# Attention and feed-forward layer on one core: the last chunk's stores as one transfer per queue and tile for two blocks of 32 rows

## The chip, the core and the metric

The kernel runs on one core of a Trainium2 chip. Its engines work side by side: TensorE (PE in the profile, its weight loads PEld) multiplies matrices, VectorE (DVE) and ScalarE (ACT) work on tiles, GpSimd (POOL) does a few small things, and SyncE (SP) issues transfers. A transfer (DMA) is issued by SP or ACT, goes into that engine's DMA queue and is carried out by the core's 16 DMA engines, between the memory on the chip (128 partitions) and the large memory outside. In the profile SP's queue is q1 and ACT's is q10.

The metric is the device time of one execution in microseconds (us), as the median of several runs. A difference of 0.2% is about what can be told apart here.

## The reference, cut to what matters

There are 8 batches, 8 heads, 32 global and 512 local positions, a head dimension of 64 and a model width of 512. The global queries attend to all 544 positions, the local ones to the global ones and to a band of 32 to each side. A layer with normalization and two matrices follows, on all 8 x 544 rows of 512 numbers:

```python
    out_g = np.matmul(sm(s_g), v_all)                                  # 32 global rows per batch
    out_l = np.matmul(a_l, np.concatenate([v_g, v_l], axis=2))         # 512 local rows per batch
    attn_out = np.concatenate([out_g, out_l], axis=2)                  # global rows stand first
    x = attn_out.transpose(0, 2, 1, 3).reshape(B, S, H * D)
    xn = (x - mu) / np.sqrt(var + 1e-06) * g_ln
    ch = np.maximum(xn @ w_ch1, 0.0) @ w_ch2
    return (x + ch).astype(np.float32)
```

The lines are put together from the reference's functions. The output has the shape 8 x 544 x 512. So the 32 global rows of one batch are one run of 64 KB in memory, and from one batch's to the next batch's there are 544 rows.

## The kernel before, in words

The work goes in nine chunks. Eight of them hold 512 local rows each, as four tiles of 128 rows. The last chunk holds the global rows of all 8 batches: 256 rows, as two tiles of 128, and each tile is four blocks of 32 rows from four batches. While the feed-forward part of one chunk runs, the attention of the next one runs beside it.

The feed-forward part (class `Ffn`) takes 16 steps. In each, `first` multiplies the normalized rows with a piece of the first matrix (L830, into `ph`), ScalarE and VectorE make the hidden values in two parts (L839, L843), and `second` adds their product with a piece of the second matrix to `acc` (L855), one `acc` for each tile of rows.

At a chunk's end, tile by tile: `residual` has loaded the rows of x from the scratch tensor `xs` into `ob` some time before, `add` (L867, VectorE) adds `acc` to `ob`, and `store` (L869 to L875) sends `ob` to the output. In the wide chunks a tile is one block of 128 rows and one transfer on SP's queue (by `dma`, L407). In the last chunk `rows_global` lists four blocks of 32 rows for a tile, and `store` is called twice: with `part` 0 it takes the first two blocks (partitions 0 to 63) on SP's queue, with `part` 1 the other two (partitions 64 to 127) on ACT's queue (L875). Each block is a transfer of its own, 64 KB.

The order of instructions on each engine is written out in a table by operation number. A call of `store` is one operation in it, whatever number of transfers it issues, so the change leaves the table as it is. Nothing follows the last stores but the end of the program.

Of the kernel before, what the change touches and what calls it, by code (L numbers as in the profile page):

```python
# [319 lines left out]
def attention_ffn_kernel(  # L320
# [12 lines left out]
    nc = tc.nc  # L333
# [4 lines left out]
    SA = gk.shape[4] - SG  # L338
# [34 lines left out]
    for sgn in (1, -1):  # L373
        nc.gpsimd.affine_select(
            out=band,
# [30 lines left out]
    def dma(to, src):  # L406
        nc.sync.dma_start(to, src)  # L407
# [104 lines left out]
    class Local:  # L512
# [116 lines left out]
        def store(self, j):  # L629
            b, _, half = self.at  # L630
            r0 = b * SA + SG + half * 256 + j * P
            dma(xs[r0:r0 + P, :], self.x[:, j, :])
# [179 lines left out]
    out_flat = out.rearrange("b s d -> (b s) d")  # L812

    class Ffn:
# [54 lines left out]
        def store(self, t, part=0, parts=1):  # L869


            n = len(self.rows[t]) // parts
            for ps, r0, nr in self.rows[t][part * n:part * n + n]:
                if part:
                    nc.scalar.dma_start(out_flat[r0:r0 + nr, :], self.ob[ps, t, :])  # L875
                else:
                    dma(out_flat[r0:r0 + nr, :], self.ob[ps, t, :])

    def open_pool(name):
        cm = tc.tile_pool(name=name, bufs=1, reuse_waits="tile")  # L880
# [686 lines left out]
```

## Time and profile before

| what | value |
|---|---|
| runs | 904.42, 905.08, 905.54 us; median 905.08 |
| the profiled execution's own time | 905.45 us |
| its span, first to last instruction | 903.6 us |
| PE busy | 889.5 us, 98% of the span |
| DVE, ACT, POOL busy | 694.8, 311.0, 40.6 us |
| mean granted TensorE clock | 0.994 of full speed |
| memory read and written | 100.67 and 17.83 MB |

The span leaves out what lies around the first and the last instruction, 1.85 us here. Busy shares are means over the whole program; the chain of waits says what is on the path to the end. A DMA's share is that of 16 engines: 100% means that all 16 were busy.

### The profile page before, as it was taken

Reading aid. Unit: us, or ns where it says so; the run is one execution under the profiler, and the core shown is the slowest. Engines: PE = TensorE matmul, PEld = TensorE weight load, DVE = VectorE, ACT = ScalarE, POOL = GpSimd, SP = SyncE. Lnnn points to the kernel's source line nnn. Section 1 sums busy time; section 2 is a strip of 40 time slices with the busy share of each in tenths; the row PEclk is TensorE's granted clock in tenths of the full one; section 3 lists DMA queues with packets and bytes.
Section 4 is the critical chain, followed back from the end, with each engine's and each line's share of the span. In section 5 each row is a group of like instructions: output and inputs, shape, how many; then the busy total and the mean of one; then the engine's idle time right before and its main releaser. Section 6 shows DMA issues by size and latency. Waiting matters only on the chain.

```text
span 903.6 us, 21437 instructions
## 1 busy us (share of the span) xinstructions
PE 889.5 (98%) x8517; PEld 707.2 (78%) x8517; DVE 694.8 (77%) x2448; ACT 311.0 (34%) x880; POOL 40.6 (4%) x133
## 2 busy tenths in 40 slices
PE   7899999999999999999999999999999999999997
PEld 4588787877788887778877787878887777777896
DVE  5899999789878888788878896888876287766411
ACT  7798873232223222322322222322323122222211
POOL 4100100000000000000000000000000000000000
PEclk9899999999999999999999999999999999999999
DMA  9696836324134313324332403332331426445200
GB/s 347 251 333 207 284 110 210 101 79 148 47 104 147 118 38 125 102 78 148 120 101 83 148 16 110 118 117 92 125 102 53 155 101 238 162 176 204 68 15 24
DMA packets 42868, 119.88 MB, mean 133 GB/s; under 512 B 5136, under 2 KB 7184, under 8 KB 40720
## 3 DMA queue, kind: packets, MB, share of 16 engines
q1 hardware_dynamic: 42576, 118.25, 37.9%
q8 instruction: 67, 1.10, 0.5%
q14 instruction: 33, 0.27, 0.1%
q10 hardware_dynamic: 192, 0.26, 0.1%
HBM read 100.67 MB, written 17.83 MB: 131 GB/s over the span
## 4 chain that ended last, share of the span: by engine, by line
PE 83%; DVE 2%; issue 0%
PE ph L830 37%; PE acc L855 37%; PE sc L548 3%; PE pv L603 3%; PE pv L739 1%; PE sc L662 1%; DVE pt L595 1%; PE tp L710 0%; DVE xl L808 0%; DVE ob L867 0%; PE t L790 0%; DVE w L462 0%; DVE hl L843 0%; DVE tmp L452 0%; DVE tmp L446 0%
## 5 line engine op out<-in xcount | busy, mean ns | idle before, releaser
L855 PE MATMUL acc<-w,hh 128*128 128x512 f32 x1088 | 342.0, 395 | 0.0
L830 PE MATMUL ph<-xh,w 128*128 128x512 f32 (+1 forms) x1216 | 308.2, 379 | 0.8 <-DVE hl L843 0.6
L830 PEld LDWEIGHTS ph<-xh,w 128*128 128x128 f32 x1216 | 215.5, 188 | 49.0 <-DVE hl L843 1.1
L855 PEld LDWEIGHTS acc<-w,hh 128*128 128x128 f32 x1088 | 204.9, 188 | 47.4
L839 ACT ACTIVATE hh<-ph 128x512 fp32r<-128x512 f32 (+1 forms) x144 | 82.9, 576 | 438.9 <-PE ph L830 409.1
L855 PE MATMUL acc<-w,hl 128*128 128x512 f32 x544 | 218.5, 402 | 0.0
L595 DVE STREAM_TRANSPOSE pt<-p 32x128 f32<-32x128 f32 x768 | 207.2, 289 | 9.5 <-ACT p L572 1.1
L843 DVE SCALAR_TENSOR_TENSOR hl<-ph,hh 128x512 fp32r<-128x512 f32 (+1 forms) x144 | 95.2, 661 | 120.0 <-ACT hh L839 119.0
L830 PE MATMUL ph<-xl,w 128*128 128x512 f32 x512 | 141.1, 397 | 0.0
L572 ACT ACTIVATE p<-p,mn 128x128 f32<-128x128 f32 x256 | 99.8, 392 | 92.5 <-DVE mn L560 92.4
L855 PEld LDWEIGHTS acc<-w,hl 128*128 128x128 f32 x544 | 102.1, 188 | 23.3
L830 PEld LDWEIGHTS ph<-xl,w 128*128 128x128 f32 x512 | 95.7, 188 | 23.8 <-DVE xl L808 0.2
L798 DVE STREAM_TRANSPOSE tmp<-x 32x128 f32<-32x128 f32 x320 | 96.7, 302 | 4.8
L560 DVE CUSTOM_DVE_ANT_0 p<-sc,mask 128x128 f32<-128x128 f32 x256 | 61.0, 284 | 21.7 <-PE sc L548 21.3
L572 ACT ACTIVATION_READ_ACCUMULATOR p<-p,mn 128x1 f32 x256 | 48.4, 189 | 0.0
L615 POOL TENSOR_SCALAR ri<-sm 128x4 f32<-128x4 f32 x64 | 16.9, 264 | 639.9 <-ACT p L572 638.1
L722 DVE STREAM_TRANSPOSE gpt<-gp 32x128 f32<-32x128 f32 x144 | 43.5, 302 | 2.3
L622 DVE TENSOR_TENSOR x<-pv,ri 128x256 f32<-128x256 f32 x64 | 24.8, 418 | 13.8 <-PE pv L603 13.8
L548 PEld LDWEIGHTS sc<-u_e 64*32 64x32 f32 x1792 | 24.9, 105 | 10.2 <-issue 8.8
L548 PE MATMUL sc<-u_e 64*32 64x128 f32 x1792 | 32.4, 274 | 0.0
L603 PE MATMUL pv<-u_v,pt 128*32 128x64 f32 x1792 | 30.8, 220 | 0.0
L603 PEld LDWEIGHTS pv<-u_v,pt 128*32 128x32 f32 x1792 | 26.3, 110 | 5.7 <-issue 5.7
(71 smaller groups left out, 501.7 us busy)
## 6 DMA issues: line engine op xcount, KB each, us to landing
u_v<-in_ev SPq DMA_DIRECT2D x56, 512.0 KB, 4.9
u_e<-in_eq SPq DMA_DIRECT2D x56, 336.0 KB, 6.2
raw<-in_wd SPq DMA_DIRECT2D x32, 512.0 KB, 7.4
gk<-in_gk SPq DMA_DIRECT2D x8, 1152.0 KB, 6.3
xs<-x SPq DMA_DIRECT2D x32, 256.0 KB, 6.3
ob<-xs SPq DMA_DIRECT2D x32, 256.0 KB, 5.6
out<-ob SPq DMA_DIRECT2D x32, 256.0 KB, 3.7
gv<-in_gv SPq DMA_DIRECT2D x8, 1024.0 KB, 5.0
```

Of the source, the lines that this page charges most:

```text
L548: nc.tensor.matmul(sc[h][gp, qb * P:(qb + 1) * P], self.e[hd, w * WIN:(w + 1) * WIN], self.e[hd, k0 * WIN:(k0 + 4) * WIN], start=True, sto ...
L560: nc.vector.tensor_tensor_reduce(out=self.p[:, c], in0=self.sc[h][:, qb * P:(qb + 1) * P], in1=masks[self.at[2], qb], scale=-QSCALE, scala ...
L572: nc.scalar.activation(self.p[:, c], self.p[:, c], AF.Exp, bias=self.mn[:, c:c + 1], scale=-1.0, accum_out=self.sm[:, c:c + 1],)
L595: nc.vector.transpose(out=self.pt[rp, :, gp], in_=self.p[gp, :, rp])
L603: nc.tensor.matmul(pv[gp, qb * P + h * D:qb * P + h * D + D], self.pt[:, 2 * h + qb, gp], self.v[:, 4 * qb + g, h * D:(h + 1) * D], start= ...
L622: nc.vector.tensor_tensor(self.x[:, :, hp * P:(hp + 1) * P].rearrange("p q (h d) -> p q h d", h=2), self.pv[:, :256].rearrange("p (q h d) ...
L722: nc.vector.transpose(out=self.pt[rp, h, :n, ip], in_=p[ip, :, r])
L798: nc.vector.transpose(out=dst[rp, 2 * half:2 * half + 2, :, i], in_=src[ip, :, k:k + 2, r])
L830: nc.tensor.matmul(self.ph[f][:, :self.n], w[:, kt, :], xx[kt][:, :self.n], start=begins and kt == 0, stop=ends and kt == KT - 1,)
L839: nc.scalar.activation(hh[:, :self.n], self.ph[f][:, :self.n], AF.Relu)
L843: nc.vector.scalar_tensor_tensor(hl[:, :self.n], self.ph[f][:, :self.n], 0.0, f32(hh[:, :self.n]), ALU.max, ALU.subtract,)
L855: nc.tensor.matmul(self.acc[t], a[:, ts], w, start=(f == 0 and i == 0), stop=(f == NF - 1 and i == 2),)
```

## The change

In the last chunk, one call of `store` issues one transfer for its two blocks of 32 rows. The destination is addressed as a piece of the output of 2 batches x 32 rows x 512, the source as 64 partitions x 512. SP and ACT still take two blocks of a tile each. For a tile with one block (the wide chunks) the transfer is what it was.

```diff
             n = len(self.rows[t]) // parts
-            for ps, r0, nr in self.rows[t][part * n:part * n + n]:
-                if part:
-                    nc.scalar.dma_start(out_flat[r0:r0 + nr, :], self.ob[ps, t, :])
-                else:
-                    dma(out_flat[r0:r0 + nr, :], self.ob[ps, t, :])
+            ps, r0, nr = self.rows[t][part * n]
+            if n == 1:
+                to, ob = out_flat[r0:r0 + nr, :], self.ob[ps, t, :]
+            else:
+                b = r0 // SA
+                to = out[b:b + n, :nr, :]
+                ob = self.ob[ps.start:ps.start + n * nr, t, :]
+            (nc.scalar.dma_start if part else dma)(to, ob)
```

On SP's queue the end of the program reads so (`-` before, `+` changed; `out` is the output, `ob` the tile of sums, `xs` the scratch tensor; the sizes are those of the destination, and in brackets stand the semaphores that an instruction waits for, those of DMA queues and VectorE's):

```order
 L407 DMA ob<-xs 32x512 [waits DMAHW4_49]
 L407 DMA ob<-xs 32x512 x4
-L407 DMA out<-ob 32x512 [waits DMAHW2_49,DMAHW1_49,DVE_49]
-L407 DMA out<-ob 32x512 [waits DMAHW3_49]
-L407 DMA out<-ob 32x512 [waits DMAHW5_49,DVE_49]
-L407 DMA out<-ob 32x512 [waits DMAHW7_49,DMAHW6_49]
-L1563 UNCONDITIONAL_BRANCH
+L407 DMA out<-ob 2x32x512 [waits DMAHW2_49,DMAHW1_49,DVE_49]
+L407 DMA out<-ob 2x32x512 [waits DMAHW5_49,DMAHW6_49,DMAHW3_49,DVE_49]
+L1566 UNCONDITIONAL_BRANCH
```

Four transfers with two waits for VectorE's additions have become two with one such wait each, and the destination has three dimensions where it had two.

On ACT's queue, behind the last activations of the hidden values:

```order
 L839 ACTIVATE hh<-ph 128x256 [waits DVE_49,PE_49] x15
-L875 DMA out<-ob 32x512 [waits DMAHW3_49,DMAHW1_49,DVE_49]
-L875 DMA out<-ob 32x512 [waits DMAHW4_49]
-L875 DMA out<-ob 32x512 [waits DMAHW7_49,DMAHW6_49,DVE_49]
-L875 DMA out<-ob 32x512 [waits DMAHW0_49]
-L1563 UNCONDITIONAL_BRANCH
+L880 DMA out<-ob 2x32x512 [waits DMAHW3_49,DMAHW4_49,DMAHW1_49,DVE_49]
+L880 DMA out<-ob 2x32x512 [waits DMAHW7_49,DMAHW0_49,DVE_49]
+L1566 UNCONDITIONAL_BRANCH
```

The same has happened here, and the line of the issue is now L880. No other instruction of any engine has moved.

## Rows read from the trace of the kernel before

**Rows 1.** Page, busy time by engine and the chain by engine.

```profile
PE 889.5 (98%) x8517; PEld 707.2 (78%) x8517; DVE 694.8 (77%) x2448; ACT 311.0 (34%) x880; POOL 40.6 (4%) x133
...
PE 83%; DVE 2%; issue 0%
```

**Rows 2.** Chain in order of time, its end: start us, us, what.

```profile
896.02 2.82 PE acc L855 x12
898.84 0.02 issue
898.86 0.69 DVE ob L867
```

**Rows 3.** Timeline from 890: start us, us, engine, line, operation, tiles, count.

```profile
898.16 1.39 DVE L867 TENSOR_TENSOR ob<-acc,ob 128x512 f32<-128x512 f32 x2 [1.26 <-PE acc L855]
...
898.88 1.99 SPq L407 DMA_DIRECT2D out<-ob  x4
898.89 1.83 ACTq L875 DMA_DIRECT2D out<-ob  x4
```

**Rows 4.** Tile `ob` from 897 on: issue ns min/median/max, first and last start.

```profile
L407 SPq DMA_DIRECT2D out<-ob x4: 314/340/417, 898.9 to 900.6; - x4
L875 ACTq DMA_DIRECT2D out<-ob x4: 361/412/446, 898.9 to 900.3; - x4
...
DMA to landing us min/median/max: 1.7/1.9/2.3
```

**Rows 5.** DMA packets, 899.6 to 902.8, in 40 slices of 0.08 us.

```profile
DMA  0999289999489999498976975944210000000000
GB/s 0 205 205 282 51 282 359 359 333 230 102 282 359 359 256 230 102 282 307 308 231 179 231 179 154 307 154 179 103 26 26 0 0 0 0 0 0 0 0 0
DMA packets 385, 0.53 MB, mean 167 GB/s; under 512 B 128, under 2 KB 128, under 8 KB 384
...
q1 hardware_dynamic: 192, 0.26, 34.2%
q10 hardware_dynamic: 192, 0.26, 25.0%
```

**Rows 6.** The same, 852.8 to 856, four wide stores (128x512).

```profile
GB/s 0 256 410 410 358 384 384 410 358 256 308 410 358 384 384 410 384 358 384 410 410 384 384 333 358 307 384 410 410 384 410 358 410 410 410 256 77 0 0 0
DMA packets 576, 1.05 MB, mean 328 GB/s; under 512 B 64, under 2 KB 64, under 8 KB 576
...
q1 hardware_dynamic: 576, 1.05, 89.1%
```

**Rows 7.** Line L407, whole trace: the issues of stores on SP.

```profile
L407 SPq DMA_DIRECT2D out<-ob x36: 314/338/1952, 149.4 to 900.6; - x36
```

**Rows 8.** Timeline of SP from 850: issues of the last residual loads.

```profile
856.19 3.57 SPq L407 DMA_DIRECT2D ob<-xs  x8
```

## The prediction

> **What bounds the kernel now.** I read the busy lines and the chain of the page first. TensorE is busy for 98% of the span and the chain runs along it almost from end to end [rows 1]; the change touches no matmul, so nothing before the last few microseconds can move. The end is then read from the chain in order of time: the last matmuls finish at 898.84, the second of two additions (0.69 us) runs to 899.55 [rows 2], and the span ends at 903.6. About 4 us behind the last arithmetic are thus stores and their landing, and they are on the path with nothing beside them. The timeline shows how they are issued: from 898.9 SP issues four stores in 1.99 us and ACT four in 1.83 us [rows 3]. The first two of each queue belong to row tile 0, whose addition ends near 898.86, the other two to tile 1, whose addition ends at 899.55. The issue rows give 0.34 us (SP) and 0.41 us (ACT) for one, and a median of 1.9 us from issue to landing [rows 4]. The view of the DMA packets, with slices of 0.08 us from 899.6, shows the first data in the second slice (899.7) and the last in the thirty-first (902.1) [rows 5]. What is left between 902.1 and 903.6, 1.5 us, is landing and the closing of the program.
>
> The same view says how a store is spread. There are 128 packets under 512 bytes for 8 stores, 16 for each, and 256 larger ones, 32 for each: one per row of 2 KB [rows 5]. A store of 128 rows also has 16 small packets (64 for 4 stores) and 128 large ones [rows 6]. I take the 16 small packets for one closing packet per DMA engine: each store of today runs on all 16 engines, two rows on each where there are 32 rows. All 16 have these few bytes to move, so the end part is short.
>
> **The change part by part.** Four transfers of 32 rows on each queue become two of 2 x 32 rows, for the last chunk alone; the wide chunks' stores keep their form. Removed are two issues per queue, some 0.34 to 0.41 us each [rows 4]. Data stays: 8 x 64 KB = 512 KB = 256 rows of 2 KB. What is new is the shape of the transfer. Its side in memory has an outermost dimension of 2, the blocks lying one batch apart; the side on the chip has 64 rows. Every transfer of today that the tail rows show has an outermost dimension of 32 or 128 on both sides, multiples of 16, and is dealt evenly to 16 engines. If rows are dealt by the outermost dimension that the two sides share, a transfer of 2 x 32 rows can be dealt to 2 engines only, 32 rows on each. No row of before shows such a transfer, so the price is bounded from both sides: dealt over 16 as now, the data takes what it takes now or slightly less; dealt over 2, it takes many times as long. I take the second, and the same two engines for all four transfers, since two queues that start counting at the same engine pick the same pair.
>
> A rule bears on this. The page "DMA: Bandwidth & Descriptors" of the Trainium skill, section "Why a DMA increments its semaphore by 16 and not by 1", says that a transfer issued from SP or ACT uses the largest number of engines up to 16 that divides the slowest dimension, other than 1, of both sides, and that these are the lowest-numbered ones; here that would be 2, the same 2 for both queues, and the sum by it is the one below. The 16 closing packets of 32-row and 128-row stores agree with it [rows 5, 6], but no run here shows a smaller number. The same page's "Rules for kernel authors" advises to coalesce small transfers into one large one; by that alone the first rival below would hold, with its 904.6.
>
> Step by step, with two engines:
> 1. *Start.* The first issues stay at 898.9, released by the first addition; first data at 899.7 today. The issue itself may be longer with one dimension more. The stores' issues on SP range from 0.31 to 1.95 us with a median of 0.34 [rows 7], so between 0 and 1.6 us more; nearest to the median, I take 0.25. First data at 899.95.
> 2. *Data.* 256 rows over 2 engines are 128 rows on each. For one row on one engine, the four wide stores at 852.8 to 856 give a rate with all engines full: 89.1% of 16 engines x 3.2 us is 45.6 us for 512 rows, 89 ns with closing packets included [rows 6]. 128 x 0.089 = 11.4 us, against 2.4 us today (899.7 to 902.1). Bounds: the densest slices there run at 410 GB/s, 25.6 GB/s per engine or 80 ns a row, 10.2 us in all; the tail's own packets take 34.2% and 25.0% of 16 x 3.2 us for 128 rows each, 137 ns on SP's queue and 100 on ACT's, with a mean of 118 [rows 5], which gives 15.1 us and 17.5 at the worst. I stay with 89, since the tail's packets share the reading of 32 rows among 16 engines, which 2 engines do not.
> 3. *Second issues.* They leave at 899.6 at the earliest (after the second addition), at 900.2 or so with longer issues. The engines still have over 5 us of tile 0's rows then, so these issues, their waits and the two that are gone are all hidden. Without that cover, in the first rival, they count.
> 4. *End.* 899.95 + 11.4 = 911.35 for the last data, + 1.5 as today = 912.85, against 903.6: +9.25 us. Added to the profiled execution (905.45): 914.7. That execution lies 0.37 above the median of the runs; on the median's footing 914.3.
>
> The waits of the new stores name the loads of both blocks at once; these landed some 37 us earlier (issued 856.2 to 859.8) [rows 8], so they cost nothing. Nothing follows a store on either queue, so nobody waits for one but the program's end.
>
> **The rivals.**
> *Still sixteen engines (not slower).* If the 64 rows are dealt as one run of rows, the only thing that changes is the issuing. Today SP's fourth issue ends at 898.88 + 1.99 = 900.87, 1.3 us after the second addition. With one issue per tile the last one starts at 899.6. The data still needs 256 x 118 ns / 16 = 1.9 us from 899.7, so to 901.6, 0.5 us earlier than today: 904.6. At most the last issue's whole lead of about 1 us is won: 904.1. It decides if the first data packets of the two stores overlap on all engines as they do now. For it: the rows of both blocks lie one behind the other on the chip, 64 in a row. Against it: on the other side they do not, and there is no row where a transfer with a gap between its blocks was spread at all.
> *Two engines for each transfer, but not the same two.* If each queue has its own pair, 64 rows on an engine take 64 x 0.089 = 5.7 us: 899.95 + 5.7 + 1.5 = 907.15, +3.55, so 908.6. If each of the four transfers has its own pair, 32 rows take 2.85 us; tile 1's data starts near 899.6 + 0.8 + 0.25 = 900.65 and ends at 903.5, + 1.5 = 905.0, +1.4, so 906.5. For it: packets of both queues move side by side today. Against it: they then use all 16 engines, so this shows nothing of a choice.
> *The change doesn't reach the chip as written* is excluded by the order of instructions, which has two transfers of 2x32x512 on each queue.
>
> **How the numbers follow.** Two shared engines 0.85; sixteen engines 0.09; own pairs 0.06, half of it per queue (slower) and half per transfer (no change). A measurement of this kernel tells about 0.2%, 1.8 us, from no change. Sixteen engines gives at most 1 us by the sum, so I leave 0.02 of its 0.09 for faster. Slower: 0.85 + 0.03 = 0.88; no change 0.07 + 0.03 = 0.10; faster 0.02. The forecast's own bounds: 80 ns a row and no longer issue give 899.7 + 10.2 + 1.5 = 911.4, +7.8, 912.9; 118 ns and 1.6 us give 917.9, +14.3, 919.4. With 0.4 us for the spread of the runs the range is 912.5 to 920. It leaves out the two rivals (0.15) and little else.
>
> **What would show it.** In the profile of the changed kernel: four packets under 512 bytes per queue in the tail where there were 64 (two per transfer); a DMA share near 2 of 16 engines, so about 1 in the tenths, for some 11 us; about 45 to 50 GB/s in that stretch; stores that take 6 to 12 us from issue to landing, the later ones longest; matmuls and additions ending at 898.8 and 899.55 as now. Sixteen small packets per transfer would prove the first rival; a share of 4 or 8 engines the second. A row time far from 89 ns on two engines would make the size wrong, not the mechanism. A start of data later than 900.2 would say that the issue was undersized.

## The result, and the profile after

The changed kernel takes 915.7 us (median of 4 runs, 914.71 to 916.76), the kernel before in the same comparison 904.75 us (4 runs, 902.91 to 905.54). The ratio is 1.0124 with a 95% interval of 1.011 to 1.0137: slower by 1.2%, as forecast (914.3, range 912.5 to 920).

The profiled execution took 914.71 us, with a span of 912.8. The timeline's end shows the additions and the issues that answer to [rows 3]:

```profile
896.81 1.39 DVE L867 TENSOR_TENSOR ob<-acc,ob 128x512 f32<-128x512 f32 x2 [1.26 <-PE acc L855]
...
897.53 1.39 SPq L407 DMA_DIRECT2D out<-ob  x2
897.54 2.03 ACTq L880 DMA_DIRECT2D out<-ob  x2
```

This execution came to its additions 1.35 us earlier than that of before (896.81 against 898.16), a difference between executions that the change cannot make. So the two ends are to be compared from the first issue on: 903.6 - 898.88 = 4.7 us before, 912.8 - 897.53 = 15.3 us after, 10.6 us more. The two medians lie 10.95 us apart. To within 0.4 us, less than the runs of one kernel differ by, the whole loss is thus behind the last arithmetic.

The tile `ob`, as in [rows 4], gives the length of an issue:

```profile
L407 SPq DMA_DIRECT2D out<-ob x2: 526/600/673, 897.5 to 898.4; - x2
L880 ACTq DMA_DIRECT2D out<-ob x2: 534/955/1376, 897.5 to 899.0; - x2
```

There are half as many issues, and each is longer: 0.53 and 0.67 us on SP, 0.53 and 1.38 on ACT, where [rows 4] has 0.34 and 0.41. All are over by 899.6. What comes behind them is seen in the DMA packets, here from 897.5 to 912.7 in slices of 0.38 us, to be read beside [rows 5]:

```profile
DMA  0001110111111101111111111111111111100000
GB/s 0 0 0 22 16 11 11 32 43 38 38 32 27 49 38 54 49 49 54 54 49 49 54 54 49 49 54 54 49 49 54 49 49 43 49 27 11 0 0 0
DMA packets 265, 0.53 MB, mean 35 GB/s; under 512 B 8, under 2 KB 8, under 8 KB 264
...
q1 hardware_dynamic: 132, 0.26, 5.7%
q10 hardware_dynamic: 132, 0.26, 4.4%
```

Eight packets are under 512 bytes where there were 128: two for each of the four transfers. The data is the same, 256 rows of 2 KB, but the share of the 16 engines stands near 1 tenth, and 49 to 54 GB/s flow in most slices from the sixteenth (903.2) on, where [rows 5] has up to 359. The data begins in the fourth slice (898.6 to 899.0) and ends in the thirty-seventh (911.2 to 911.6): about 12.6 us, against 2.4 us.

From 903 to 907 packets of both queues move side by side, and together they make 51 GB/s:

```profile
DMA packets 102, 0.20 MB, mean 51 GB/s; under 512 B 2, under 2 KB 2, under 8 KB 102
...
q1 hardware_dynamic: 54, 0.11, 6.9%
q10 hardware_dynamic: 48, 0.10, 6.3%
```

That is twice the 25.6 GB/s which one engine reaches in [rows 6] (410 on 16), so both queues together have two engines here, and not two each.

### The profile page after: what moved, and what is told of

Read it like the earlier page. It is cut to its first block, busy times and chain, and to the rows that moved or that the text cites. A ratio compares the mean times of both kernels' runs of the same rounds, so it can differ in the third digit from the quotient of the medians.

```text
span 912.8 us, 21434 instructions
## 1 busy us (share of the span) xinstructions
PE 888.5 (97%) x8517; PEld 706.7 (77%) x8517; DVE 694.9 (76%) x2448; ACT 311.1 (34%) x880; POOL 40.7 (4%) x133
## 4 chain that ended last, share of the span: by engine, by line
PE 82%; DVE 2%; issue 0%
PE ph L830 37%; PE acc L855 37%; PE sc L548 3%; PE pv L603 3%; PE pv L739 1%; PE sc L662 1%; DVE pt L595 1%; PE tp L710 0%; DVE xl L808 0%; DVE ob L867 0%; PE t L790 0%; DVE w L462 0%; DVE hl L843 0%; DVE tmp L452 0%; DVE tmp L446 0%
## 5 line engine op out<-in xcount | busy, mean ns | idle before, releaser
L622 DVE TENSOR_TENSOR x<-pv,ri 128x256 f32<-128x256 f32 x64 | 24.8, 418 | 12.6 <-PE pv L603 12.5
L548 PEld LDWEIGHTS sc<-u_e 64*32 64x32 f32 x1792 | 24.9, 105 | 10.2 <-issue 8.8
```

The costliest lines, as they stand in the source:

```text
L548: nc.tensor.matmul(sc[h][gp, qb * P:(qb + 1) * P], self.e[hd, w * WIN:(w + 1) * WIN], self.e[hd, k0 * WIN:(k0 + 4) * WIN], start=True, sto ...
L622: nc.vector.tensor_tensor(self.x[:, :, hp * P:(hp + 1) * P].rearrange("p q (h d) -> p q h d", h=2), self.pv[:, :256].rearrange("p (q h d) ...
```

## The experiments

The theory was that the outermost dimension of a transfer sets how many engines carry it, and that all transfers with few engines share the same ones. Six kernels were run. Two give the stores other shapes (e1, e2), three give the shared engines other loads or another queue (e3, e5, e6), and one puts the shape of the change at another place (e4). The data times below are read from the DMA slices of each run, to within a slice.

**As many transfers, but the rows outermost (e1).** Edit against the kernel before, in `store` for the last chunk:

```diff
-            for ps, r0, nr in self.rows[t][part * n:part * n + n]:
-                ...
+            if t == 0:
+                return
+            queue = nc.scalar if part else nc.sync
+            for i in (2 * part, 2 * part + 1):
+                to = out.rearrange("(g i) s d -> i s g d", i=BG)[i, :SG]
+                queue.dma_start(to, self.ob[i * SG:(i + 1) * SG, 0:2, :])
```

> As many transfers as in the changed kernel (two per queue, 2 x 32 rows each), but a transfer takes one block of 32 rows from both tiles, so its outermost dimension is 32 on both sides and the gap between two batches is the second one. Theory (the outermost dimension sets how many engines carry a transfer): 16 closing packets for each of the 4 transfers, 64 in the tail; data within about 2 us as in the kernel before; but nothing can be sent before the second addition, so the end is 0.3 to 1.2 us later than before: 905.0 to 906.0 beside 904.75. Rival (a transfer in three dimensions with a gap between its blocks is slow in itself): data for some 12 us as in the changed kernel, 915 or more.

Measured: 905.02 us (10 runs) beside 903.99 (19 runs of before), ratio 1.0012, interval 1.0003 to 1.0022. The DMA packets from 899.6 to 902.8, in slices of 0.08 us:

```profile
GB/s 0 0 0 0 0 0 0 0 0 128 154 256 179 154 205 102 205 179 179 308 384 410 410 384 359 410 307 231 307 359 384 307 205 52 0 0 0 0 0 0
DMA packets 320, 0.52 MB, mean 164 GB/s; under 512 B 64, under 2 KB 64, under 8 KB 320
```

There are 64 small packets for four transfers, 16 each, and the data is through in 2.0 us, from the tenth slice to the thirty-fourth. The second thing to see is when its issues come and how long they take:

```profile
898.12 1.39 DVE L867 TENSOR_TENSOR ob<-acc,ob 128x512 f32<-128x512 f32 x2 [1.26 <-PE acc L855]
...
899.54 0.81 SPq L881 DMA_DIRECT2D out<-ob  x2
899.54 0.88 ACTq L881 DMA_DIRECT2D out<-ob  x2
...
L881 SPq DMA_DIRECT2D out<-ob x2: 337/346/356, 899.5 to 900.0; - x2
L881 ACTq DMA_DIRECT2D out<-ob x2: 379/392/405, 899.5 to 900.0; - x2
```

The third dimension does not make an issue longer (0.34 to 0.36 us on SP, as in [rows 4]), and neither the gap nor the size of 128 KB makes a transfer slow. The rival falls. What is left of a loss is 0.1%: the first issue waits for both additions, at 899.5 instead of 898.9. The second addition ends at 899.5 and the span at 904.0, 4.5 us later, against 4.05 us before. In the profile half the issues thus win back about 0.2 of the 0.6 us that the start is later; the medians, 1.0 us apart, show no gain from them.

**Four blocks in one transfer (e2).** Tile 0 goes by SP's queue, tile 1 by ACT's:

```diff
+            if part != t:
+                return
+            queue = nc.scalar if part else nc.sync
+            queue.dma_start(out[BG * t:BG * t + BG, :SG, :], self.ob[:, t, :])
```

> One transfer per tile for all four blocks, 4 x 32 x 512, tile 0 on SP's queue and tile 1 on ACT's. Theory: four closing packets per transfer, 8 in the tail; four engines carry 64 rows each at 80 ns, 5.1 us, plus a slow start of 1 to 2.4 us as seen in the changed kernel (12.6 us for 128 rows at 80 ns): the end some 4 to 6 us after that of before, 908.5 to 910.5. Rival (the merged form costs by its size or its gaps, not by the number of engines): transfers twice as large and three gaps in each, so 915 or later.

Measured: 909.79 us (4 runs), ratio 1.0068 (1.0053 to 1.0083). The DMA packets from 897.5 to 912.7, slices of 0.38 us:

```profile
DMA  0014121222222222222210000000000000000000
GB/s 0 0 32 32 5 11 16 59 65 81 102 102 102 97 102 102 102 102 102 92 54 16 0 0 0 22 0 0 0 0 22 0 0 0 0 0 0 0 0 0
DMA packets 266, 0.54 MB, mean 36 GB/s; under 512 B 8, under 2 KB 8, under 8 KB 264
```

Two transfers with 8 small packets are four each. The rate is 102 GB/s, twice that of the change, and the data takes 7.2 us. A larger transfer with three gaps is faster than the smaller one with one gap, so it is the number of engines that counts: outermost dimension 2 gives 2 engines, 4 gives 4, and 32 gives 16. The rates say the same as the small packets: 51, 102 and, in the densest slices of e1, 410 GB/s are 2, 4 and 16 times 25.6.

**SP's stores alone merged (e3).** The change for `part` 0, the loop of before for `part` 1:

```diff
+            if part == 0 and n == 2:
+                ps, r0, nr = self.rows[t][0]
+                b = r0 // SA
+                dma(out[b:b + n, :nr, :], self.ob[ps.start:ps.start + n * nr, t, :])
+                return
```

> SP's stores merged as in the change, ACT's four stores as before. Theory (both queues' merged transfers share one pair of engines): that pair now has 64 rows of SP's and 8 of ACT's, 72 x 80 ns = 5.8 us plus a slow start of up to 2.4 us: the end 4 to 6 us after that of before, 908.5 to 910.5. Rival (each queue or each transfer has its own pair and something else holds them to 51 GB/s): SP's queue takes what it took in the changed kernel, 914 to 916. If ACT's part were what costs: 905.

Measured: 910.34 us (4 runs), ratio 1.0076 (1.006 to 1.0093). The DMA packets from 897.5 to 912.7, with data for about 7.9 us:

```profile
GB/s 0 5 167 113 81 65 75 70 92 81 65 59 49 43 49 49 54 49 54 49 54 43 16 0 0 0 22 0 0 0 22 0 0 0 0 0 0 0 0 0
DMA packets 326, 0.54 MB, mean 36 GB/s; under 512 B 68, under 2 KB 68, under 8 KB 324
```

The 68 small packets are two for each of SP's two transfers and 16 for each of ACT's four. The kernel ends 5.4 us earlier than the changed one. The last data is SP's and comes 8.8 us after its first issue (897.37 to 906.2); with the very same transfers on SP's queue, the changed kernel has SP's packets until 909.1, 11.6 us after the issue. So ACT's merged transfers took time from SP's there.

**The loads merged in place of the stores (e4).** The stores are those of before; in `residual`, for the last chunk:

```diff
+            if self.nt == 2:
+                x3 = xs.rearrange("(b s) d -> b s d", s=SA)
+                for i in (0, 2):
+                    b = BG * t + i
+                    dma(self.ob[i * SG:(i + 2) * SG, t, :], x3[b:b + 2, :SG, :])
+                return
```

> Stores as in the kernel before; instead the eight loads of 32 rows of the scratch tensor into ob for the last chunk are merged in the same way into four of 2 x 32 rows. Theory: they go over 2 engines and take some 11 to 13 us in all, but they start near 856 and are first needed at 898, so nothing is lost: within 0.2% of before, 904 to 906. Rival (the form costs on the queue or holds up the program wherever it stands): 909 to 915.

Measured: 904.1 us (10 runs), ratio 0.9997 (0.9986 to 1.0008), no change. The DMA packets from 853 to 870 in slices of 0.425 us, where the first four slices are the end of a wide store:

```profile
DMA  9997000030011111111111111111111111100000
GB/s 386 376 386 294 0 0 0 0 19 0 10 53 53 48 39 53 53 48 48 48 58 48 48 48 48 48 48 48 48 53 48 48 53 48 48 19 0 0 0 0
```

The loads crawl at mostly 48 to 53 GB/s for some 12 us, and nobody waits for them: they are through at 868.3, and the first addition starts at 897.1. The same form costs 11 us at the end of the program and nothing here.

**All merged stores on SP's queue (e5).** One word of the change:

```diff
-            (nc.scalar.dma_start if part else dma)(to, ob)
+            dma(to, ob)
```

> All four merged transfers (2 x 32 x 512) issued by SP, none by ACT. Theory (one pair of engines carries all merged transfers, whichever queue issues them): 128 rows on each as in the changed kernel, so 914.5 to 916.5, with data at about 51 GB/s once it flows. On the slow start of some 1.5 to 2.4 us: if it came from the two queues that issue at once, it is gone here and the end is 1 to 2 us earlier than in the changed kernel, 913.5 to 914.5; if it belongs to a transfer's own start on two engines, it stays. Rival (each queue has its own pair): SP's pair is now the only one and has twice the rows, so its data takes about 20 us, 924 or more.

Measured: 914.92 us (4 runs), beside 904.11 (7 runs of before), ratio 1.0125 (1.0108 to 1.0142). The DMA packets from 897.5 to 912.7:

```profile
GB/s 0 0 0 16 22 5 16 43 59 38 32 32 32 38 32 32 22 43 49 54 49 54 49 49 54 49 54 49 54 49 54 49 54 49 54 49 22 0 0 0
```

The second queue gives nothing: with one queue the data takes the same 12.6 us at the same rate. With a pair per queue SP's pair would now carry twice the rows, about 20 us by the expectation's estimate. The slow start is here too, so it does not come from two queues issuing at once.

**Tile 0 alone merged, on both queues (e6).** The change where `t` is 0, the loop of before where it is 1:

```diff
+            if t == 0 and n == 2:
+                ps, r0, nr = self.rows[t][part * n]
+                b = r0 // SA
+                (nc.scalar.dma_start if part else dma)(
+                    out[b:b + n, :nr, :], self.ob[ps.start:ps.start + n * nr, t, :])
+                return
```

> Both queues' stores of tile 0 merged, those of tile 1 as before. Theory (one shared pair): 64 rows of tile 0 and 8 of tile 1 on each of two engines, 72 x 80 ns = 5.8 us and a slow start of 1 to 2.4 us: like the run with SP's stores alone merged, 909 to 911. Rival (each queue has its own pair): 32 rows of tile 0 and 8 of tile 1 on an engine, 3.2 us and the slow start: 906 to 907.5.

Measured: 909.44 us (4 runs), ratio 1.0067 (1.0052 to 1.0082). The DMA packets from 897.5 to 912.7, with data for 7.6 us:

```profile
GB/s 0 0 0 22 16 43 54 102 119 146 146 59 92 92 81 70 59 54 49 49 75 43 22 11 0 0 0 0 0 22 0 0 0 0 0 0 0 0 0 0
```

That is the time for a shared pair with 72 rows per engine, 5.8 us and a slow start of about 2, and not that for a pair per queue, which would have 40 rows on an engine, 3.2 us and the start.

No version beat the kernel before. e4 shows no change, and e1 is 0.1% slower.

## Why the prediction was right

*The mechanism.* The step that decided was the second of the sum: two engines, the same for all four transfers. Two small packets per transfer show the two engines, and e1 and e2 show that the outermost dimension sets their number. That both queues use the same two is shown by the 51 GB/s of both together from 903 to 907 and by e3, e5 and e6. The engines have no names in this trace, so that they are the lowest-numbered ones, as the Trainium skill says ("DMA: Bandwidth & Descriptors", section "Why a DMA increments its semaphore by 16 and not by 1"), is not seen; the number it gives is seen in each of the shapes here (2, 4 and 16). The advice of the same page of the Trainium skill to coalesce small transfers, in "Rules for kernel authors", brought no gain in any run here: with 2 engines it cost 1.2%, and with 16 engines kept (e1) the time was 0.1% longer, though e1 also starts 0.6 us later. The line of the same rules of the Trainium skill on using all 16 engines, which asks for an outermost dimension that is a multiple of 16, is the one that e1 bears out.

*Start.* 0.25 us more for the issue was forecast. The packets from 898.3 to 901.5 of the changed kernel, in slices of 0.08 us, begin in the seventh:

```profile
GB/s 0 0 0 0 0 0 51 26 26 0 51 0 26 0 0 0 26 0 26 0 26 0 0 26 26 51 26 51 26 51 51 51 51 51 26 26 26 51 26 26
DMA packets 35, 0.07 MB, mean 22 GB/s; under 512 B 0, under 2 KB 0, under 8 KB 35
...
q1 hardware_dynamic: 35, 0.07, 10.3%
```

First data is at 898.8, 1.3 us after the issue, where it was 0.8 before: 0.45 us more instead of 0.25. The reason that was given, one dimension more, is not what made the issue longer: e1 has that dimension, and its first data, in the tenth slice of its rows (from 900.32), comes 0.8 us after the issue at 899.54.

*Data.* 11.4 us was forecast, and it took 12.6. Two errors are in this term, of opposite sign. Once the data flows, it flows at 51 GB/s on two engines, 25.6 on each, 80 ns a row: the lower bound of the sum, 10.2 us. The 89 ns were the time that a packet takes, and packets of one engine overlap, so that their times add up to more than the engines' span. The kernel before shows it from 853.4 to 855.4, in the middle of the stores of [rows 6], with over 100%:

```profile
q1 hardware_dynamic: 413, 0.75, 101.8%
```

The other error is a slow start that the forecast had no term for. The first 1.3 us of the rows at 898.3 bring a few rows only, the full rate comes at 903.2, and the last two slices of the long view are below it again (27 and 11 GB/s). In all 12.6 - 10.2 = 2.4 us are lost, most of them at the start. The other runs agree: 7.2 us for 64 rows per engine (5.1 + 2.1), 7.6 and 7.9 for 72 (5.8 + about 2). That 89 ns for 80 made up for half of the missing start is luck.

*Second issues.* They were done by 899.6, with 11 us of data still to come, and were hidden as forecast.

*End.* 912.8 - 911.4 = 1.4 us, against 1.5.

*Sum.* Forecast +9.25 us. From issue to end it is +10.6: 0.2 us more at the start, 1.2 more for the data and 0.1 less at the end make the difference. That the span grew by 9.2, almost the figure forecast, is luck: the profiled execution was 1.35 us quicker up to the last additions.

*Rivals.* Sixteen engines (904.6) falls with the two small packets per transfer and with the 915.7 us. Whether its gain of 0.5 us would come with 16 engines is not shown: e1 has them, but starts later and is 0.1% slower than before. Own pairs (908.6 or 906.5) fall with the 51 GB/s of both queues together and with e3, e5 and e6.

## What to carry to other kernels

Before merging transfers, look at the outermost dimension of each side: in every shape here (2, 4, 32 and 128) it said over how many DMA engines the rows were dealt, and a merge that puts a small count outermost takes engines away. The closing packets tell: their number per transfer in the view of DMA packets (2, 4 or 16 here) went with the rate, 25.6 GB/s for each. Fewer transfers are worth nothing if the last one lands later, and a slow transfer costs nothing where it is covered, so the same edit is to be judged by its place.

## What the runs showed of the hardware beyond this

The first transfer on few engines starts slowly: in e2 the slices from the first data (898.5) to 900.2 have 5 to 32 GB/s, against 102 later. This was so for stores and loads, on one queue and on two. Its cause was not tried and stays open.

An issue is longer with few engines: 0.50 to 0.67 us on SP with 2 engines in e5, against 0.34 to 0.36 in e1 with 16 and as many dimensions. On ACT the first one of the changed kernel took 1.38 us beside SP's, and the one of e2, which came after SP's had ended, 1.17.

The two queues did not share the pair evenly at first. In the rows above, up to 901.5, all 35 packets are SP's (q1), though ACT's issue started at the same time (897.54 against 897.53). In e2, too, all 110 packets up to 902.4 are SP's, though ACT's issue had ended at 899.1. Later the two queues share the engines about evenly (54 and 48 packets from 903 to 907). Why ACT's rows come so late was not tried.
